# Attention units issued in pairs of a pooled and a local one, batch 1's pooled units spread among local ones, and 41 zero products in place of 76

## The chip, the cores and the metric

The kernel is one program on one core of a Trainium2 chip. The metric is device time in microseconds (us), from the start of the launch to its end. Every run is an execution of the whole program; three runs of the kernel before are shown, and one more execution was profiled. In the rows PE is the matrix engine (TensorE), PEld its weight loads, DVE the vector engine, ACT the scalar engine, POOL the GpSimd engine and SP the engine that issues the DMAs.

## The reference

Three layers run one after the other on 2 x 576 tokens of 512 numbers (8 heads of 64).

```python
# attention, per batch and head
q_d, k_d, v_d = means over groups of 4 positions          # 144 pooled positions
out_d   = softmax(q_d k_d^T / 8) v_d                       # pooled part, repeated 4 times
out_loc = softmax(where(|i-j| < 4, q k^T / 8, -1e9)) v     # local part, a band of 7 keys
x = out_up + out_loc                                       # (1152, 512)
# first FFN
h = x @ w_in;  g = softplus(h);  y = g @ w_out             # 512 -> 2048 -> 512
# 8 experts, each over all tokens
P = exp(y @ w_gate - max), 8 rounds of row and column normalisation
out = sum_e P[:, e] * (relu(y @ w1[e]) @ w2[e])            # 512 -> 1024 -> 512
```

## The kernel before, in words

**The stages.** Attention for both batches comes first, then the first FFN (lines 424 and 464), then the gate and the experts (lines 514 and 563). The experts begin at 337 us and take the rest of the time. The weights of the first FFN arrive as pairs of 32-bit words and are converted in `from_double` (line 115: three ACT, five DVE and one POOL instruction for each of eight pieces); `prep` starts one piece.

**Attention.** There are 8 pooled units and 10 local units for each batch. A pooled unit covers 72 pooled queries of two heads, a local unit 116 (the last ones 112) queries of four heads with a window of 122 keys. A unit has four steps, s1 to s4:

- s1: scores into a bank of PSUM, `pd` (two products over 64 rows, line 284) or `pl` (a mask product in bf16, line 339, and four products over 64 rows, line 347); then DVE finds the negated maximum `nm` (line 270) and ACT the exponentials `e` (line 273).
- s2: transposes of `e` on PE (`ptd` line 299, `ptl` line 359), copied to SBUF by ACT.
- s3: products with the values (`pvd` line 308, `pvl` line 367), then on DVE the sum `rsd`/`rsl`, its reciprocal `rrd`/`rrl` and the scaled result `uld`/`ull` (lines 316 to 320, 373 to 377).
- s4: a transpose back (`pxd` line 325, `pxl` line 383). A pooled unit's result is kept in `upT`; a local unit adds it on DVE (line 389) and POOL writes x (lines 400, 401).

The 64 rows of a head lie in the upper or the lower half of the array: a pooled unit p uses half `p // 2`, a local unit g half `g`. All these banks come from one pool of 6 buffers (`psa`, line 205); the banks of the first FFN and of the zero products come from a pool of 2 (`psm`, line 204).

**The order.** `emit` (line 715) takes units one at a time and issues s1 of the newest unit, s2 of the unit two places earlier, s3 four and s4 six places earlier. Batch 0 and batch 1 each run as four pooled units, then local and pooled ones in turn, then the remaining local ones (line 735). Other work is hung on a place in this list (lines 756 to 764): the loads of batch 1, the pooling of its q and k (`pool_qk`), the `prep` calls, and pieces of the first FFN, the last six of which come after the last unit begins. A scheduler then sets the order of each engine's instructions from this program order and its own estimate of times; every engine runs its list in order.

**Zero products.** `warm` (line 186) multiplies a zero tile of 128 x 128 with 512 zero columns on PE; nothing reads the result. There are 17 at the start, then one behind each of the first 23 steps and behind every second step up to the 95th, 76 in all.

**Batch 1's values.** `load_vd` (line 251) loads v in groups of four positions (`vr`, two DMAs issued by SP), and adds them in two steps (`vs`, line 260, and `vd`, line 262), on DVE for batch 0 and on POOL for batch 1. Each of DVE and POOL waits in its list where such an addition stands until the transfer has landed.

Of the kernel before, what the change touches and what calls it, by code (L numbers as in the profile page):

```python
# [47 lines left out]
AT = (0, 256)  # L48
A11, A12, A22, S1, S2, S3, S4 = range(7)
B11, B21, B22, T1, T2, T3, T4 = range(7)  # L50
STEP = 2
WARM, JALL, JN, NJ = 17, 24, 2, 96
GP = 80
SCALE = 0.125
assert SCALE == D**-0.5
# [20 lines left out]
class Net:  # L76
# [143 lines left out]
    def pool_qk(self, b, p):  # L220

        nc = self.nc

        def sums(t, nm):
            s = self.atp.tile([P, G, 2], F32, tag="ks", name=f"s{nm}{b}{p}", bufs=2)
            v = t.rearrange("p (g f) -> p g f", f=POOLF)
            nc.gpsimd.tensor_tensor(s, v[:, :, 0:2], v[:, :, 2:4], ALU.add)
            nc.gpsimd.tensor_tensor(d, s[:, :, 0], s[:, :, 1], ALU.add)

        q = self.qT[b, p]  # L230
        d = self.atp.tile([P, G], F32, tag="qd", name=f"qd{b}{p}", bufs=NPAIR)
        if b == 0:
            nc.vector.tensor_reduce(
                out=d, in_=q.rearrange("p (g f) -> p g f", f=POOLF), op=ALU.add, axis=AX.X
            )
            nc.scalar.activation(q, q, AF.Copy, scale=SCALE)
        else:
            sums(q, "q")
            nc.gpsimd.tensor_scalar(q, q, SCALE, None, ALU.mult)
        self.qd[b, p] = d  # L240
        d = self.atp.tile([P, G], F32, tag="kd", name=f"kd{b}{p}", bufs=NPAIR)
        sums(self.kT[b, p], "k")
        nc.gpsimd.tensor_scalar(d, d, SCALE / (POOLF * POOLF), None, ALU.mult)
        self.kd[b, p] = d

    def load_vw(self, b, t):
        w = self.vwp.tile([P, H, DA], F32, tag="vw", name=f"vw{b}{t}")
# [3 lines left out]
    def load_vd(self, b):  # L251
        nc = self.nc
        vd = self.atp.tile([GH, 2, H, DA], F32, tag="vd", name=f"vd{b}", bufs=2)
        nc.gpsimd.memset(vd[:, :, :, D:DA], 1.0)
        for hf in range(2):
            r = self.rawp.tile([GP, POOLF, DM], F32, tag="raw", name=f"vr{b}{hf}")
            nc.sync.dma_start(out=r, in_=self.a["vp"][b, hf].rearrange("p (f d) -> p f d", f=POOLF))
            s = self.convp.tile([GH, 2, DM], F32, tag=("ch", "cs")[hf], name=f"vs{b}{hf}", bufs=1)
            e = nc.vector if b == 0 else nc.gpsimd
            e.tensor_tensor(s, r[:GH, 0:2], r[:GH, 2:4], ALU.add)  # L260
            sv = s.rearrange("p f (h d) -> p f h d", h=H)
            e.tensor_tensor(vd[:, hf, :, 0:D], sv[:, 0], sv[:, 1], ALU.add)
        self.vd[b] = vd
        self.upT[b] = self.atp.tile([P, NPAIR, G], F32, tag="upT", name=f"upT{b}", bufs=2)

# [10 lines left out]
    def pooled(self, b, hf, p):  # L276
        nc, ident = self.nc, self.ident
        st = {}
        r = p // 2 * D

        def s1():
            ps = self.psa.tile([P, 512], F32, tag="a", name="pd")[:GH, : 2 * G].rearrange("p (j k) -> p j k", j=2)
            for j in range(2):
                nc.tensor.matmul(
                    ps[:, j],
                    lhsT=self.qd[b, (2 * p + j) % 4][r : r + D, hf * GH : (hf + 1) * GH],
                    rhs=self.kd[b, (2 * p + j) % 4][r : r + D, :],
                    start=True,
                    stop=True,
                )  # L290
# [12 lines left out]

        def s3():
            ps = self.psa.tile([P, 512], F32, tag="a", name="pvd")[:GH, : 2 * DA].rearrange("p (j d) -> p j d", j=2)
            for j in range(2):
                for kh in range(2):
                    nc.tensor.matmul(
                        ps[:, j],
                        lhsT=st["pt"][:, j, kh],  # L310
                        rhs=self.vd[b][:, kh, 2 * p + j],
                        start=(kh == 0),
                        stop=(kh == 1),
                    )
# [12 lines left out]

        return [s1, s2, s3, s4]

    def local(self, b, t, g):  # L330
        nc, ident = self.nc, self.ident
# [2 lines left out]
        nq = min(QT, S - QT * t)  # L334
        mv = OFF.index(QT * t - w0)

        def s1():
            ps = self.psa.tile([P, 512], F32, tag="a", name="pl")[:nq, : 4 * KW].rearrange("p (j k) -> p j k", j=4)
            nc.tensor.matmul(
                ps,  # L340
                lhsT=self.identb[:nq, :nq],
                rhs=self.mask[:nq, mv : mv + 1, :].to_broadcast([nq, 4, KW]),
                start=True,
                stop=False,
            )
            for j in range(4):
                nc.tensor.matmul(
                    ps[:, j],
                    lhsT=self.qT[b, j][g * D : (g + 1) * D, QT * t : QT * t + nq],
                    rhs=self.kT[b, j][g * D : (g + 1) * D, w0 : w0 + KW],  # L350
                    start=False,
                    stop=(j == 3),
                )
            st["e"] = self.softmax_exp(ps, 4, nq, KW, "l")
# [47 lines left out]
                n += m  # L402
            self.ends.append((dve.ins, st["act"].ins))

        return [s1, s2, s3, s4]


    def banks(self, n, name):
# [283 lines left out]
    def run(self):  # L692
# [19 lines left out]
        for t in range(3):  # L712
            self.load_vw(0, t)

        def emit(items, rest):

            live = []
            n = 0
            tail = [y for x in zip([None] * (3 * STEP), rest) for y in x] + rest[3 * STEP :]
            for it in [*items, *tail]:  # L720
                if callable(it):
                    it()
                    continue
                live = [it, *live][: 3 * STEP + 1]
                for k, u in enumerate(live[::STEP]):
                    if u is not None:
                        u[k]()
                        n += 1
                        if n < JALL or n % JN == 0 and n < NJ:
                            self.warm(1)  # L730

        def units(b):
            pooled = [self.pooled(b, hf, p) for hf in range(2) for p in (0, 2, 1, 3)]
            local = [self.local(b, t, g) for t in range(NQT) for g in range(2)]
            return pooled[:4] + [u for z in zip(local, pooled[4:]) for u in z] + local[4:]

        def load_second():

# [9 lines left out]
        def prep(n, lag):  # L748

            with ExitStack() as st:  # L750
                for ins in self.ends[-1 - lag]:
                    st.enter_context(self.tc.issue_after(ins))
                self.prep(n)


        at = {1: [load_second], 9: [load_rest]}
        for p in range(NPAIR):
            at.setdefault(13 + p, []).append(lambda p=p: self.pool_qk(1, p))
        for n, lag, u in zip(range(2 * NFT), (1, 1, 0, 0), (14, 18, 23, 29)):
            at.setdefault(u, []).append(lambda n=n, lag=lag: prep(n, lag))  # L760
        one, two, after = self.l1(0, 0, 1), self.l2(0, 0, 1), self.l1(0, 1, 1)
        for m, u in zip(one + two[:2], (22, 24, 26, 28, 30, 32)):
            at.setdefault(u, []).append(m)
        at[36] = [after[0], after[1], two[2], after[2], after[3], two[3]]
        seq = []
        for n, u in enumerate(units(0) + units(1)):
            seq += at.get(n, []) + [u]

        emit(seq, at[36])
        first = {(0, 0), (0, 1)}  # L770
        stack.close()

# [144 lines left out]
```

## Time and profile before

| what | us |
|---|---|
| median of the three runs | 1096.75 |
| the three runs | 1095.97, 1096.75, 1122.32 |
| the profiled execution, its own time | 1097.38 |
| its span, first to last instruction | 1095.5 |
| PE busy in the span | 1066.1 (97%) |
| DVE busy | 783.6 (72%) |
| ACT busy | 433.8 (40%) |
| POOL busy | 233.1 (21%) |
| attention's last product on PE begins | 125.8 |
| experts' first product on PE begins | 337.1 |

Busy time is the time in which an engine had an instruction under way; products on PE are pipelined, so the time that one takes from PE is read from its start to the start of the next, not from its busy column. The granted clock of PE (PEclk) is a share of full speed: 1.00 is 2.4 GHz, 0.50 is 1.2 GHz. In a row of a timeline "x4" says how many instructions of the same kind stand there together; a product of 32-bit floats is two passes, so "x8" of `pl` are the four products of one unit. The brackets at the end of a row say how long the engine stood idle before it, and what ended that.

### The profile page before, as it was taken

What the parts mean: (1) busy time and instruction counts of PE and PEld (TensorE: products, weight loads), DVE (VectorE), ACT (ScalarE), POOL (GpSimd) and SP (SyncE); (2) the same over time, 40 slices, a digit from 0 to 9 for tenths busy, and PEclk for the clock granted to TensorE, in tenths of its full rate; (3) what the DMA queues carried; (4) which work ended last, traced back from release to release, by engine and by line L of the source; (5) the groups of instructions that cost most, each with busy time, mean ns of one, the idle gap of its engine ahead of it and who ended that gap; (6) DMA issues with size and microseconds to landing.
All of it is one profiled execution on the core that took longest, in us unless ns stands there. A gap on an engine that the chain in (4) does not pass through costs nothing.

```text
span 1095.5 us, 16149 instructions
## 1 busy us (share of the span) xinstructions
PE 1066.1 (97%) x6444; PEld 966.7 (88%) x6444; DVE 783.6 (72%) x1430; ACT 433.8 (40%) x803; POOL 233.1 (21%) x254
## 2 busy tenths in 40 slices
PE   9999889999979999999999999999999999999998
PEld 5888779999969898989989898998989989899897
DVE  4788699999778676958567495774947658486562
ACT  4777667685653341314223141231413314132130
POOL 4972322222064311112021120211102011120000
PEclk9989999999999999999999999999999999999999
DMA  9431033222011111112111121111111111110003
GB/s 284 160 106 59 1 119 113 78 77 77 1 63 54 39 39 39 40 40 76 39 39 39 39 78 39 39 39 39 64 53 39 39 39 43 58 56 1 1 1 86
DMA packets 12906, 63.98 MB, mean 58 GB/s; under 512 B 1632, under 2 KB 1888, under 8 KB 6368
## 3 DMA queue, kind: packets, MB, share of 16 engines
q1 hardware_dynamic: 12832, 62.97, 17.5%
q8 instruction: 50, 0.82, 0.3%
q14 instruction: 24, 0.20, 0.1%
HBM read 60.60 MB, written 2.36 MB: 57 GB/s over the span
## 4 chain that ended last, share of the span: by engine, by line
PE 71%; DVE 6%; issue 1%; ACT 1%; POOL 0%; DVEq 0%
PE po L563 36%; PE pu L514 31%; PE py L464 2%; PE ph L424 2%; DVE l L442 1%; DVE yp L476 0%; DVE acc L584 0%; DVE ch L129 0%; DVE l L443 0%; DVE r L441 0%; DVE a L165 0%; DVE w L180 0%; DVE h L445 0%; DVE cm L126 0%; DVE T L505 0%
## 5 line engine op out<-in xcount | busy, mean ns | idle before, releaser
L563 PE MATMUL po<-w,h 128*128 128x512 f32 x1728 | 396.2, 390 | 0.0
L563 PEld LDWEIGHTS po<-w,h 128*128 128x128 f32 x1728 | 323.4, 188 | 66.5
L514 PE MATMUL pu<-T,a 128*128 128x320 f32 (+1 forms) x2688 | 355.0, 293 | 2.3 <-DVE v L536 1.0
L514 PEld LDWEIGHTS pu<-T,a 128*128 128x128 f32 x2688 | 351.7, 188 | 4.2 <-DVE v L536 1.2
L585 DVE SCALAR_TENSOR_TENSOR acc<-po,prob,acc 128x512 f32<-128x512 f32 x126 | 94.3, 749 | 175.3 <-PE po L563 175.2
L526 ACT ACTIVATE h<-c 128x256 fp32r<-128x256 f32 (+1 forms) x256 | 108.9, 443 | 182.3 <-DVE c L536 181.8
L158 POOL TENSOR_TENSOR s<-raw 128x256 f32<-128x256 f32 x32 | 32.1, 1002 | 537.8 <-DVE a L165 533.8
L179 ACT CAST w<-raw 128x1024 fp32r<-128x1024 f32 x32 | 33.7, 1053 | 276.6 <-PE po L563 270.0
L527 DVE SCALAR_TENSOR_TENSOR h<-c,h 128x256 fp32r<-128x256 f32 (+1 forms) x256 | 125.5, 505 | 1.5 <-ACT h L526 0.9
L464 PE MATMUL py<-h,w 128*128 128x384 f32 x576 | 109.7, 347 | 11.1 <-DVE h L445 5.4
L424 PE MATMUL ph<-x,w 128*128 128x384 f32 x576 | 107.6, 343 | 9.1 <-ACT cm L125 4.7
L464 PEld LDWEIGHTS py<-h,w 128*128 128x128 f32 x576 | 103.8, 194 | 13.9 <-DVE h L445 6.9
L424 PEld LDWEIGHTS ph<-x,w 128*128 128x128 f32 x576 | 102.2, 192 | 11.1 <-issue 5.0
L135 POOL TENSOR_TENSOR w<-cs,ch 128x1024 fp32r<-128x1024 f32 x16 | 42.8, 2676 | 111.8 <-DVE ch L134 72.9
L536 DVE TENSOR_TENSOR c<-v,pu 128x320 f32<-128x320 f32 (+1 forms) x128 | 57.8, 452 | 9.5 <-PE pu L514 6.3
L180 DVE TENSOR_TENSOR w<-raw,w 128x1024 fp32r<-128x1024 f32 x32 | 41.3, 1291 | 32.3 <-ACT w L179 32.3
L165 DVE TENSOR_TENSOR a<-s,a 128x1024 fp32r<-128x1024 f32 x32 | 39.8, 1244 | 1.7 <-ACT a L164 1.7
L534 ACT COPY p<-pu 128x256 f32<-128x256 f32 x64 | 25.1, 393 | 33.9 <-PE pu L514 32.3
L164 ACT CAST a<-s 128x1024 fp32r<-128x1024 f32 x32 | 33.4, 1045 | 3.6 <-POOL s L161 3.6
L441 DVE SCALAR_TENSOR_TENSOR r<-r,e 128x768 f32<-128x768 f32 (+1 forms) x28 | 27.4, 979 | 9.4 <-ACT l L440 9.4
L165 DVE TENSOR_TENSOR a<-raw,a 128x768 fp32r<-128x768 f32 x32 | 30.5, 957 | 3.6 <-ACT a L164 3.6
L536 DVE TENSOR_TENSOR v<-u,pu 128x256 f32<-128x256 f32 x64 | 29.0, 453 | 4.2 <-PE pu L514 1.3
(124 smaller groups left out, 1066.7 us busy)
## 6 DMA issues: line engine op xcount, KB each, us to landing
raw<-in_w SPq DMA_DIRECT2D x48, 1024.0 KB, 4.9
vw<-in_vw SPq DMA_DIRECT2D x10, 260.0 KB, 2.7
vr<-in_vp SPq DMA_DIRECT2D x4, 640.0 KB, 10.6
k<-in_k SPq DMA_DIRECT2D x8, 288.0 KB, 5.5
q<-in_q SPq DMA_DIRECT2D x8, 288.0 KB, 6.3
out<-acc SPq DMA_DIRECT2D x5, 256.0 KB, 2.0
out<-acc SPq DMA_DIRECT2D x8, 128.0 KB, 2.3
maskf<-in_mask SPq DMA_DIRECT2D x1, 183.0 KB, 5.8
```

What stands on the lines that cost most here:

```text
L135: nc.gpsimd.tensor_tensor(w[:, 1], s, h, ALU.mult)
L165: nc.vector.tensor_tensor(w[:, 1, lo:hi], src, split(w[:, 0, lo:hi]), ALU.subtract)
L179: nc.scalar.copy(w[:, 0], raw)
L180: nc.vector.tensor_tensor(w[:, 1], raw, split(w[:, 0]), ALU.subtract)
L424: nc.tensor.matmul(ps[:, i], lhsT=wv[:, a, k, fo : fo + P], rhs=x[:, b, k], start=(n == 0), stop=(n == 3 * KD - 1),)
L464: nc.tensor.matmul(ps[:, a], lhsT=w[:, i, d * P : (d + 1) * P], rhs=h[:, j, f], start=(n == 0), stop=(n == 3 * NFT - 1),)
L514: nc.tensor.matmul(ps, lhsT=w[:, x, a, k], rhs=t[:, y, b, k], start=(m == 0), stop=(m == 5))
L526: nc.scalar.activation(hi, src, AF.Relu)
L527: nc.vector.scalar_tensor_tensor(lo, src, 0.0, split(hi), ALU.max, ALU.subtract)
L536: nc.vector.tensor_tensor(to, src, ps, ALU.add)
L563: nc.tensor.matmul(ps, lhsT=h[i][:, f, at * P : (at + 1) * P], rhs=w[:, j], start=(n == 0), stop=(n == 3 * NFT - 1),)
L585: nc.vector.scalar_tensor_tensor(acc, ps, pe, acc, ALU.mult, ALU.add)
```

## The change

`emit` takes pairs of units. For each place it issues the mask products of the newest pair, then s1 of both its units, s2 of both units one place earlier, s3 of the pair two places and s4 of the pair three places earlier. The pairs are two of pooled units, four of a pooled and a local unit of batch 0, two of local units, eight of a pooled unit of batch 1 and a local unit (the last two local units of batch 0 and the first six of batch 1), and two of local units. In each pair of a pooled and a local unit both use the same half of the array. The pooling of batch 1's q and k, the `prep` calls and the pieces of the first FFN hang on places in the list of pairs, and none is left for after the last one. The zero products fall from 76 to 41. The additions of `load_vd` run on DVE for both batches, and the scalings of kd (both batches) and of batch 1's q run on ACT instead of POOL.

```diff
-STEP = 2
-WARM, JALL, JN, NJ = 17, 24, 2, 96
+WARM, JALL, NJ = 17, 4, 11
...
+        qd, kd = (self.atp.tile([P, G], F32, tag=t, name=f"{t}{b}{p}", bufs=NPAIR) for t in ("qd", "kd"))
         if b == 0:
...
-            nc.scalar.activation(q, q, AF.Copy, scale=SCALE)
         else:
-            sums(q, "q")
-            nc.gpsimd.tensor_scalar(q, q, SCALE, None, ALU.mult)
-        self.qd[b, p] = d
-        d = self.atp.tile([P, G], F32, tag="kd", name=f"kd{b}{p}", bufs=NPAIR)
-        sums(self.kT[b, p], "k")
-        nc.gpsimd.tensor_scalar(d, d, SCALE / (POOLF * POOLF), None, ALU.mult)
-        self.kd[b, p] = d
+            sums(q, qd, "q")
+        sums(self.kT[b, p], kd, "k")
+        nc.scalar.activation(kd, kd, AF.Copy, scale=SCALE / (POOLF * POOLF))
+        nc.scalar.activation(q, q, AF.Copy, scale=SCALE)
+        self.qd[b, p], self.kd[b, p] = qd, kd
...
-            e = nc.vector if b == 0 else nc.gpsimd
-            e.tensor_tensor(s, r[:GH, 0:2], r[:GH, 2:4], ALU.add)
+            nc.vector.tensor_tensor(s, r[:GH, 0:2], r[:GH, 2:4], ALU.add)
             sv = s.rearrange("p f (h d) -> p f h d", h=H)
-            e.tensor_tensor(vd[:, hf, :, 0:D], sv[:, 0], sv[:, 1], ALU.add)
+            nc.vector.tensor_tensor(vd[:, hf, :, 0:D], sv[:, 0], sv[:, 1], ALU.add)
...
-        return [s1, s2, s3, s4]
+        return [None, s1, s2, s3, s4]
...
-        def emit(items, rest):
+        def emit(pairs, before):
 
             live = []
...
+            for n in range(len(pairs) + 3):
+                for m in before.get(n, []):
+                    m()
+                live = [pairs[n] if n < len(pairs) else (), *live][:4]
+                for u in live[0]:
+                    if u[0]:
+                        u[0]()
+                for k, pair in enumerate(live):
+                    for u in pair:
+                        u[k + 1]()
+                    if n < JALL or n < NJ and k % 2:
+                        self.warm(1)
...
-        at = {1: [load_second], 9: [load_rest]}
-        for p in range(NPAIR):
-            at.setdefault(13 + p, []).append(lambda p=p: self.pool_qk(1, p))
-        for n, lag, u in zip(range(2 * NFT), (1, 1, 0, 0), (14, 18, 23, 29)):
-            at.setdefault(u, []).append(lambda n=n, lag=lag: prep(n, lag))
+        (p0, l0), (p1, l1) = units(0), units(1)
+
+        pairs = [(p0[0], p0[1]), (p0[2], p0[3]), *zip(p0[4:], l0), (l0[4], l0[5]), (l0[6], l0[7])]
+        pairs += [*zip(p1, l0[8:] + l1), (l1[6], l1[7]), (l1[8], l1[9])]
+
+        before = {1: [load_second], 5: [load_rest]}
+        for p, n in enumerate((4, 4, 5, 6)):
+            before.setdefault(n, []).append(lambda p=p: self.pool_qk(1, p))
+        for n, lag, u in zip(range(2 * NFT), (1, 1, 0, 0), (7, 9, 11, 14)):
+            before.setdefault(u, []).append(lambda n=n, lag=lag: prep(n, lag))
         one, two, after = self.l1(0, 0, 1), self.l2(0, 0, 1), self.l1(0, 1, 1)
...
+        order = one + two[:2] + [after[0], after[1], two[2], after[2], after[3], two[3]]
+        for m, u in zip(order, (11, 12, 13, 14, 15, 16, 17, 18, 18, 19, 20, 21)):
+            before.setdefault(u, []).append(m)
+        emit(pairs, before)
```

Three places of the engines' lists show what moves. A number behind a name says which buffer it is; "x4" stands for four in a row.

The first is PE's list in batch 0, where pooled and local units stand beside each other. Before, from the mask product of one local unit:

```order
L339 LDWEIGHTS identb
L339 MATMUL pl<-mask,identb 116x488
L347 MATMUL pl<-k_118,q_120 116x122
L347 MATMUL pl<-k_122,q_124 116x122
L347 MATMUL pl<-k_142,q_144 116x122
L347 MATMUL pl<-k_154,q_156 116x122
L359 MATMUL ptl<-ident,e 122x116 x4
L367 MATMUL pvl<-vw_189,ptls 116x65 x4
L195 LDWEIGHTS z
L195 MATMUL pz<-z 128x512
```

Of the change, one pair and the steps of the pairs before it:

```order
L335 LDWEIGHTS identb
L335 MATMUL pl<-mask,identb 116x488
L346 MATMUL pl<-k_118,q_120 116x122
L346 MATMUL pl<-k_122,q_124 116x122
L346 MATMUL pl<-k_142,q_144 116x122
L346 MATMUL pl<-k_154,q_156 116x122
L279 MATMUL pd<-kd_147,qd_146 72x144
L279 MATMUL pd<-kd_159,qd_158 72x144
L294 MATMUL ptd<-ident,e 72x72 x4
L358 MATMUL ptl<-ident,e 122x116 x4
L303 MATMUL pvd<-vd_176,ptds 72x65 x4
L366 MATMUL pvl<-vw_189,ptls 116x65 x4
```

The two products `pd` stand directly behind the four `pl` now, both over the same 64 rows, while before the 64-row products of a pooled and of a local unit were parted by full-height work; the zero products between them are gone.

The second is DVE's list where the values of batch 1 come in. Of the change, from the fifth pooled unit's sum on (`vr_484` and `vr_489` are the two transfers):

```order
L311 TENSOR_SCALAR rsd<-pvd 72x2
L255 TENSOR_TENSOR vs_486<-vr_484 72x1024
L313 RECIPROCAL rrd<-rsd 72x2
L372 TENSOR_SCALAR rsl<-pvl 116x4
L257 TENSOR_TENSOR vd_482<-vs_486 72x8x64
L315 TENSOR_TENSOR uld<-pvd,rrd 72x128
L374 RECIPROCAL rrl<-rsl 116x4
L255 TENSOR_TENSOR vs_491<-vr_489 72x1024
L376 TENSOR_TENSOR ull<-pvl,rrl 116x256
L265 TENSOR_REDUCE nm<-pl 116x4
L265 TENSOR_REDUCE nm<-pd 72x2
```

Before, POOL had these additions:

```order
L239 TENSOR_SCALAR q_208<-q_208 128x576
L260 TENSOR_TENSOR vs_461<-vr_459 72x1024
L228 TENSOR_TENSOR kd_679<-sk_680 128x144
L227 TENSOR_TENSOR sq_746<-q_214 128x288
L260 TENSOR_TENSOR vs_466<-vr_464 72x1024
L262 TENSOR_TENSOR vd_457<-vs_461 72x8x64
```

The additions `vs` and `vd` now stand in DVE's list among the maxima, reciprocals and scaled results of the units under way, where before only POOL waited for the transfers.

The third is PE's list at the first product of the first FFN (`ph`). Of the change:

```order
L335 LDWEIGHTS identb
L335 MATMUL pl<-mask,identb 116x488
L346 MATMUL pl<-k_215,q_216 116x122 x2
L346 MATMUL pl<-k_215,q_222 116x122
L346 MATMUL pl<-k_215,q_225 116x122
L279 MATMUL pd<-kd_500,qd_499 72x144
L279 MATMUL pd<-kd_583,qd_582 72x144
L294 MATMUL ptd<-ident,e 72x72 x4
L358 MATMUL ptl<-ident,e 122x116 x4
L303 MATMUL pvd<-vd_482,ptds 72x65 x4
L423 MATMUL ph<-x_94,w_668 128x384
```

The last zero product of the change is the 113th instruction of PE's list and the first `ph` the 224th; between them stand attention's products alone. Before, zero products reach to 94.0 us and the first `ph` is at 70.17 us.

## Rows read from the trace of the kernel before

**Rows 1.** Busy time by stretch; columns named in its first line.

```profile
core 0: us, PE busy (x) PEld busy (x) DVE busy (x) ACT busy (x) POOL busy (x), PEclk, DMA share, GB/s
0.00:20.00 20.00, 17.51 (x86) 7.95 (x87) 9.67 (x17) 8.17 (x19) 7.29 (x19) 1.00 0.93 270
20.00:57.00 37.00, 37.00 (x319) 30.30 (x317) 27.07 (x71) 25.65 (x75) 32.67 (x33) 1.00 0.60 190
57.00:67.50 10.50, 9.94 (x91) 7.92 (x91) 8.27 (x26) 7.45 (x19) 9.40 (x13) 1.00 0.47 152
67.50:74.30 6.80, 6.80 (x29) 5.66 (x28) 5.84 (x11) 3.32 (x9) 5.49 (x9) 0.50 0.00 0
74.30:125.80 51.50, 51.50 (x398) 45.42 (x396) 37.59 (x98) 34.51 (x94) 16.22 (x23) 1.00 0.16 53
139.00:142.70 3.70, 3.06 (x10) 3.09 (x11) 3.56 (x5) 2.16 (x3) 2.37 (x1) 0.54 0.57 237
337.00:1095.50 758.50, 752.42 (x4486) 682.72 (x4484) 509.05 (x1015) 217.19 (x423) 103.71 (x123) 1.00 0.13 43
```

**Rows 2.** All zero products: minimum, median, maximum ns, first and last start.

```profile
L195 PE MATMUL pz<-z x76: 376/381/650, 1.0 to 94.0; 128*128 128x512 bf16 x76
```

**Rows 3.** PE's timeline 30 to 34 us: start, busy, engine, line, operation, tiles.

```profile
30.64 0.37 PE L339 MATMUL pl<-mask,identb 116*116 116x488 bf16 x1
30.95 1.09 PE L347 MATMUL pl<-k,q 64*116 64x122 f32 x8
31.96 0.61 PE L359 MATMUL ptl<-ident,e 116*122 116x116 f32 x4
32.41 0.94 PE L367 MATMUL pvl<-vw,ptls 122*116 122x65 f32 x8
33.19 0.38 PE L195 MATMUL pz<-z 128*128 128x512 bf16 x1
33.41 0.36 PE L383 MATMUL pxl<-ident,ull 116*128 116x116 f32 x2
```

**Rows 4.** PE's timeline near 9 us, two row halves alternating.

```profile
8.92 0.47 PE L284 MATMUL pd<-kd,qd 64*72 64x144 f32 x4 [0.23 <-POOL kd L243]
9.32 1.68 PE L195 MATMUL pz<-z 128*128 128x512 bf16 x7
```

**Rows 5.** PE's timeline 66 to 71 us, the clock falling.

```profile
66.02 0.68 PE L284 MATMUL pd<-kd,qd 64*72 64x144 f32 x4
66.63 0.44 PE L299 MATMUL ptd<-ident,e 72*72 72x72 f32 x4
66.91 0.68 PE L308 MATMUL pvd<-vd,ptds 72*72 72x65 f32 x8
67.42 0.50 PE L383 MATMUL pxl<-ident,ull 112*128 112x112 f32 x2
67.72 0.61 PE L339 MATMUL pl<-mask,identb 116*116 116x488 bf16 x1
68.26 1.97 PE L347 MATMUL pl<-k,q 64*116 64x122 f32 x8
70.17 0.69 PE L424 MATMUL ph<-x,w 128*128 128x384 f32 x1
```

**Rows 6.** DVE's timeline, and the two landings that POOL waited for.

```profile
14.47 1.22 DVE L260 TENSOR_TENSOR vs<-vr 72x1024 f32<-72x1024 f32 x1 [2.87 <-DMA vr<-in_vp]
...
30.78 0.16 DVE L316 TENSOR_SCALAR rsd<-pvd 72x2 f32<-72x2 f32 x1 [0.80 <-PE pvd L308]
...
L260 POOLq EVENT_SEMAPHORE  x2: 17/17/17, 30.6 to 32.8; - x2
```

**Rows 7.** PE's two long waits after attention.

```profile
132.57 2.38 PE L464 MATMUL py<-h,w 128*128 128x384 f32 x12 [2.02 <-DVE l L443]
139.64 9.94 PE L424 MATMUL ph<-x,w 128*128 128x384 f32 x48 [4.69 <-ACT cm L125]
```

**Rows 8.** ACT's scaling of batch 0's q.

```profile
L236 ACT ACTIVATE q<-q x4: 682/682/684, 5.2 to 10.8; 128x576 f32<-128x576 f32 x4
```

More of the change, by code (lines that the diff above doesn't have):

```diff
@@ L222, in pool_qk, with sums @@
         nc = self.nc
-        def sums(t, nm):
+        def sums(t, d, nm):
             s = self.atp.tile([P, G, 2], F32, tag="ks", name=f"s{nm}{b}{p}", bufs=2)
@@ L230, in pool_qk @@
         q = self.qT[b, p]
-        d = self.atp.tile([P, G], F32, tag="qd", name=f"qd{b}{p}", bufs=NPAIR)
+        qd, kd = (self.atp.tile([P, G], F32, tag=t, name=f"{t}{b}{p}", bufs=NPAIR) for t in ("qd", "kd"))
         if b == 0:
             nc.vector.tensor_reduce(
-                out=d, in_=q.rearrange("p (g f) -> p g f", f=POOLF), op=ALU.add, axis=AX.X
+                out=qd, in_=q.rearrange("p (g f) -> p g f", f=POOLF), op=ALU.add, axis=AX.X
             )
-            nc.scalar.activation(q, q, AF.Copy, scale=SCALE)
         else:
-            sums(q, "q")
-            nc.gpsimd.tensor_scalar(q, q, SCALE, None, ALU.mult)
-        self.qd[b, p] = d
-        d = self.atp.tile([P, G], F32, tag="kd", name=f"kd{b}{p}", bufs=NPAIR)
-        sums(self.kT[b, p], "k")
-        nc.gpsimd.tensor_scalar(d, d, SCALE / (POOLF * POOLF), None, ALU.mult)
-        self.kd[b, p] = d
+            sums(q, qd, "q")
[3 more added lines that the diff above has]
+        self.qd[b, p], self.kd[b, p] = qd, kd
     def load_vw(self, b, t):
@@ L335, in local, with s0 @@
         mv = OFF.index(QT * t - w0)
-        def s1():
+        def s0():
             ps = self.psa.tile([P, 512], F32, tag="a", name="pl")[:nq, : 4 * KW].rearrange("p (j k) -> p j k", j=4)
+            st["ps"] = ps
             nc.tensor.matmul(
@@ L345, in s1 @@
             )
+        def s1():
+            ps = st["ps"]
             for j in range(4):
@@ L403, in s4 @@
             self.ends.append((dve.ins, st["act"].ins))
-        return [s1, s2, s3, s4]
+        return [s0, s1, s2, s3, s4]
     def banks(self, n, name):
@@ L713, in run @@
             self.load_vw(0, t)
-        def emit(items, rest):
+        def emit(pairs, before):
             live = []
[L718 to L730, printed above, removed]
+            for n in range(len(pairs) + 3):
[10 more added lines that the diff above has]
+                        self.warm(1)
+            for n in sorted(n for n in before if n >= len(pairs) + 3):
+                for m in before[n]:
+                    m()
         def units(b):
             pooled = [self.pooled(b, hf, p) for hf in range(2) for p in (0, 2, 1, 3)]
-            local = [self.local(b, t, g) for t in range(NQT) for g in range(2)]
-            return pooled[:4] + [u for z in zip(local, pooled[4:]) for u in z] + local[4:]
+            return pooled, [self.local(b, t, g) for t in range(NQT) for g in range(2)]
         def load_second():
@@ L753, in prep @@
                 self.prep(n)
-        at = {1: [load_second], 9: [load_rest]}
-        for p in range(NPAIR):
-            at.setdefault(13 + p, []).append(lambda p=p: self.pool_qk(1, p))
-        for n, lag, u in zip(range(2 * NFT), (1, 1, 0, 0), (14, 18, 23, 29)):
-            at.setdefault(u, []).append(lambda n=n, lag=lag: prep(n, lag))
-        one, two, after = self.l1(0, 0, 1), self.l2(0, 0, 1), self.l1(0, 1, 1)
[L762 to L769, printed above, removed]
+        (p0, l0), (p1, l1) = units(0), units(1)
[6 more added lines that the diff above has]
+            before.setdefault(u, []).append(lambda n=n, lag=lag: prep(n, lag))
+        one, two, after = self.l1(0, 0, 1), self.l2(0, 0, 1), self.l1(0, 1, 1)
+        order = one + two[:2] + [after[0], after[1], two[2], after[2], after[3], two[3]]
+        for m, u in zip(order, (11, 12, 13, 14, 15, 16, 17, 18, 18, 19, 20, 21)):
+            before.setdefault(u, []).append(m)
+        emit(pairs, before)
         first = {(0, 0), (0, 1)}
```

## The prediction

> **What bounds the kernel now.** I read the busy time by stretches first [rows 1]. PE is busy for 752.42 of the last 758.5 us, which the change leaves as they are; the question is what becomes of the first 140 us. From 20 to 57 us and from 74.3 to 125.8 us PE is never idle: attention is bound by PE's list there, and whatever leaves that list shortens the span. The granted clock is 1.00 in these stretches. From 67.5 to 74.3 us it is 0.50, the lower level of 1.2 GHz, and PE is still busy without a gap: the same products simply take longer. PE's timeline gives the price of each step from one start to the next [rows 3]: mask 0.31, the four `pl` 1.01, the four transposes `ptl` 0.45, `pvl` 0.78, one zero product 0.22 us. At the lower level mask and `pl` take 0.54 and 1.91 instead of 0.31 and 1.01 [rows 3, 5], 1.86 times as long. So two things decide: how many products PE is given, and at which level it runs them.
>
> The sum is made against the profiled execution, 1097.38 us; the median of the runs is 0.6 us below it, too little to correct for.
>
> **Zero products.** 35 of 76 go [rows 2], each 0.22 us of a list without gaps [rows 3]: -7.7 us. Of those that went, some filled waits in the first 20 us, where PE has 2.49 us idle [rows 1]; the bound is therefore -5.2, and I take -7.7 since nearly all stood behind 20 us or in stretches that were full.
>
> **64-row products together.** Twelve pairs now visit the 64-row form once instead of twice. What a visit costs is not a row of its own. The four passes of `pd` take 0.61 us in attention's middle [rows 5] and 0.40 where two units' products alternate between the halves [rows 4]. A saved visit lies between nothing and this difference; I take the whole of it, 12 x 0.21 = -2.5, since the entry that goes is what both rows differ by, bounds 0 and -2.5.
>
> The Trainium skill, page "TensorE: Matmul & The Clock Gate", Part 3 on packing small matmuls, says that products in different row groups of the array run at the same time. The alternating row agrees, with 0.40 against 0.61. By that rule pairs in different halves would gain about as much again; but here both units of a mixed pair use the same half, so I take nothing for it.
>
> **Batch 1's pooled units among local ones.** Before, they ran by themselves with little beside them, and PE stood 0.56 us idle from 57 to 67.5 us [rows 1]; local units now fill this: -0.6. The 6.8 us at the lower level behind it [rows 1] would be 3.7 at the higher: -3.1, if nothing of the kind comes elsewhere.
>
> **Scalings to ACT.** q takes ACT 0.68 us each [rows 8], kd has a quarter of the columns and is bounded by the same: in attention's middle four of each, at most 5.4 us, beside 25.65 us of work in 37 [rows 1]. ACT stays below its capacity; I take 0. If ACT were the last to arrive everywhere, 5.4.
>
> **Additions of batch 1's values to DVE.** This is a new wait. The transfers stand at the same place of SP's list as before, and the landings were at 30.6 and 32.8 us [rows 6]; nothing in the change speeds them. DVE's list puts the first addition behind the fifth pooled unit's `rsd`. Before, that `rsd` started at 30.78 [rows 6]. Up to there PE now has 8 zero products (1.8 us), one `pvl` (0.8) and some smaller things less, so DVE is there at about 27.8 and parks until 30.6. Behind it stand the two additions (1.22 each, [rows 6]), `rrd`, `uld`, `rrl`, `ull` and the maxima of the next pair. `ull` comes at about 35, while PE has work for 27.8 + 0.8 (`pvl`) + 0.2 (`pxd`) + 1.3 (mask, `pl`) + 0.6 (`pd`) + 2.0 (next steps), until about 32.7; then `pxd` and `pxl` wait for `uld` and `ull`. That is some 2.3 us of idle PE, 3 with the handing over between engines. Bounds: 0, if DVE comes late, and 4.5, if the maxima behind it hold up the pair that follows. I take +3. In batch 0 DVE waited in the same way, 2.87 us [rows 6], but there PE had zero products to do.
>
> **The clock.** Behind that gap the list has no zero products until the end of attention, and no full-height work of the FFN until the first `ph`. The trace of before has such a stretch once, and the clock fell at its end, 67.5, after only 0.56 us of idle in 10.5 [rows 1]; after the wait of 4.69 us it was at 0.54 too, while PE was busy for 3.06 of 3.70 us [rows 1, 7]. In the fallen stretch, attention products without a gap from 67.5 to 70.17 [rows 5] did not bring it back; it was up again at 74.3, after `ph` had begun. I therefore expect the fall soon after 32 us and the rise only behind the first `ph`. What stands between the gap and that `ph`, at full clock: eight masks with `pl` (8 x 1.32), four `pd` (0.61), four `ptd` (0.28), eight `ptl` (0.45), four `pvd` (0.51), seven `pvl` (0.78), seven `pxl` (0.30) [rows 3, 5], 27.3 us. At 1.86 times this is 23.5 more; some goes by before the fall: +22. Bounds 12 (it comes back half-way) and 24.
>
> The same page of the Trainium skill, "Why this matters for your kernels", says that idle gaps of TensorE between bursts bring the clock down. The trace agrees with it for the wait of 4.69 us but not for the fall at 67.5, where the idle time is 0.56 us in all. The measurement decides; the rule taken alone gives the rival that the clock holds.
>
> **After attention.** PE waited 2.02 and 4.69 us for DVE's and ACT's work on the FFN's first weights [rows 7]. With attention slower, that work has more time: -3, bounds 0 and -6.7.
>
> **Sum.** -7.7 - 2.5 - 0.6 - 3.1 + 3 + 22 - 3 = +8.1: 1097.4 + 8.1 = 1105.5, written as **1105 us**.
>
> **The rivals.**
> - *The clock falls and stays low to the first `ph`* (the forecast): 1105; from 1092 with the kind bounds (12 us of clock, all of the waits absorbed) to 1114 with the others (24 us, a stall of 4.5, nothing absorbed, nothing from the 64-row products). For it speaks that the one stretch of before without zero products and without `ph` lost the clock. Chance 0.60.
> - *It falls, but returns early*, since PE is busy without a gap behind the fall. For it: after the fall at 139 us PE only had to run on for the clock to return [rows 1, 7], if with full-height products. Against: 2.7 us of dense attention products did not do it [rows 5]. With 9 to 11 us of loss in place of 22: about 1093. Chance 0.12.
> - *The clock holds*, because DVE comes late enough or PSUM's six banks give PE enough to go on. For it: in the first 20 us PE idled 2.49 us and the clock stayed at 1.00 [rows 1]. Against: the zero products stood beside that idle time. Then the sum is -13.9, with the stall of 3 us -10.9: 1083 to 1086, quicker than before. It decides if the gap near 32 us is less than about half a microsecond. Chance 0.20.
> - *The clock falls already near 12 us*, where the first units start and PE waits for loads with fewer zero products to fill in. Then about 15 us more of PE's list (from there to 27.8) run at 1.86 times: +13 on the forecast, 1118, and 1121 if the later waits absorb nothing. Chance 0.08, mostly above the bound of 2%.
>
> That the change does not do what it says is a rival inside each: if putting the 64-row products together saves nothing, 2.5 us are to be added everywhere.
>
> **The numbers.** The predicted time is the likeliest case, 1105. Its own range is 1092 to 1114. The range 1081 to 1114 takes in the early return and the holding clock down to 2 us below the sum, and leaves out the last case and the far ends, about 0.15 in all. Two per cent, about what a measurement of this kernel can tell from no change, is 1075 to 1119: faster by more needs the clock to hold and 8 us more than I can find, 0.02; slower by more is the larger part of the last case and a little of the first, 0.07; within it 0.91.
>
> **What would show it.** In the trace of the change: DVE idle before `vs` from about 28 to 30.6 us with the transfer as its end; PE idle before `pxd` or `pxl` near 32 us; PEclk at 0.50 from then to shortly after the first `ph`; mask and `pl` of a pair at about 2.4 us there and at 1.3 or less at full clock; the waits at the first `py` and the second part of `ph` shorter. The prediction is wrong if PEclk stays at 1.00 between 30 and 65 us, if it is at 0.50 already before 25 us, or if PE loses time in the stretch to a wait for ACT.

## The result, and the profile after

The changed kernel takes 1111.21 us (median of four runs, 1110.91 to 1112.16), against 1097.42 before: a ratio of 1.0117 with a 95% interval of 1.0091 to 1.0143. It is 13.8 us slower; 8 had been forecast. Executions of one kernel differ here by whether, and where, the clock falls in attention: of 92 executions of the kernel before, 62 took 1094 to 1104 us and 30, at a lower mean clock, 1110 to 1139, while every one of the changed kernel took about 1111, and the ratios compare undisturbed runs.

The busy time by stretches, columns as in [rows 1]:

```profile
0.00:20.00 20.00, 16.39 (x89) 7.96 (x90) 8.97 (x17) 9.79 (x26) 4.88 (x15) 1.00 0.93 265
20.00:33.60 13.60, 12.04 (x118) 10.04 (x117) 7.74 (x25) 9.03 (x30) 7.49 (x13) 0.99 0.86 238
33.60:90.40 56.80, 56.29 (x276) 49.58 (x275) 32.92 (x83) 28.42 (x74) 20.41 (x26) 0.50 0.29 96
90.40:140.00 49.60, 48.73 (x384) 43.33 (x384) 34.51 (x91) 34.48 (x95) 15.74 (x21) 0.99 0.16 55
350.70:1109.00 758.30, 752.41 (x4485) 682.72 (x4484) 509.26 (x1015) 217.02 (x423) 102.92 (x123) 1.00 0.13 43
```

The last stretch, from the first product of the experts on, takes 758.3 us where it took 758.5 [rows 1]: all of the difference lies ahead of it, since that product comes at 350.7 us and came at 337.1. From 33.6 to 90.4 us, 56.8 us long, the clock is at 0.50 while PE is busy for 56.29 us; in finer windows the low stretch reaches from 33.2 to 91.3 us, 58 us. Before there were 6.8 such microseconds in attention.

DVE's timeline around the transfers of batch 1's values:

```profile
28.18 0.16 DVE L311 TENSOR_SCALAR rsd<-pvd 72x2 f32<-72x2 f32 x1 [0.75 <-PE pvd L303]
30.89 1.22 DVE L255 TENSOR_TENSOR vs<-vr 72x1024 f32<-72x1024 f32 x1 [2.56 <-DMA vr<-in_vp]
...
32.87 0.28 DVE L315 TENSOR_TENSOR uld<-pvd,rrd 72x128 f32<-72x128 f32 x1
...
34.27 0.41 DVE L376 TENSOR_TENSOR ull<-pvl,rrl 116x256 f32<-116x256 f32 x1
```

DVE is idle for 2.56 us with the transfer as the end of it. `rrd`, `uld` and `ull` stand behind: `uld` starts at 32.87 and `ull` at 34.27; without the wait `uld` would have followed its `rsd` within half a microsecond (0.39 us in the kernel before, 30.78 to 31.17). On PE, a pair at full clock (24.97 to 26.78) and the steps around the wait:

```profile
24.97 0.37 PE L335 MATMUL pl<-mask,identb 116*116 116x488 bf16 x1
25.27 1.09 PE L346 MATMUL pl<-k,q 64*116 64x122 f32 x8
26.20 0.65 PE L279 MATMUL pd<-kd,qd 64*72 64x144 f32 x4
26.78 0.45 PE L294 MATMUL ptd<-ident,e 72*72 72x72 f32 x4
...
29.66 0.37 PE L335 MATMUL pl<-mask,identb 116*116 116x488 bf16 x1 [0.58 <-ACT e L268]
...
31.74 0.56 PE L358 MATMUL ptl<-ident,e 116*122 116x116 f32 x4
33.29 1.20 PE L303 MATMUL pvd<-vd,ptds 72*72 72x65 f32 x8 [0.99 <-DVE rrl L374]
34.82 1.78 PE L366 MATMUL pvl<-vw,ptls 122*116 122x65 f32 x8 [0.34 <-DVE ull L376]
36.40 0.32 PE L320 MATMUL pxd<-ident,uld 72*128 72x72 f32 x1
...
36.90 0.61 PE L335 MATMUL pl<-mask,identb 116*116 116x488 bf16 x1
37.44 1.97 PE L346 MATMUL pl<-k,q 64*116 64x122 f32 x8
39.34 0.66 PE L335 MATMUL pl<-mask,identb 116*116 116x488 bf16 x1
```

In the brackets, PE stands 0.99 and 0.34 us for DVE's late results. Ahead of these it stood 0.58 us for ACT's `e`, which ran behind a scaling of q that the change had moved to ACT:

```profile
28.37 0.70 ACT L239 ACTIVATE q<-q 128x576 f32<-128x576 f32 x1
28.95 0.65 ACT L268 ACTIVATE e<-pd,nm 72x144 f32<-72x144 f32 x2
```

The `pvl` behind takes 1.58 us (34.82 to 36.40) instead of 0.78 [rows 3], and mask and `pl` of the next pair 2.44 (36.90 to 39.34) instead of 1.32: the clock has fallen at the end of the gap of 0.99 us, at 33.2; the 0.34 us come after the fall. It returns at 91.3, after `ph` has come; the `ph` at 88.72 are the first in a row:

```profile
86.35 0.67 PE L423 MATMUL ph<-x,w 128*128 128x384 f32 x1
...
88.72 3.51 PE L423 MATMUL ph<-x,w 128*128 128x384 f32 x12
92.07 0.35 PE L382 MATMUL pxl<-ident,ull 112*128 112x112 f32 x2
```

### The profile page after: what moved, and what is told of

Read it like the earlier page. It is cut to its first block, busy times and chain, and to the rows that moved or that the text cites. A ratio compares the mean times of both kernels' runs of the same rounds, so it can differ in the third digit from the quotient of the medians.

```text
span 1109.1 us, 16098 instructions
## 1 busy us (share of the span) xinstructions
PE 1080.1 (97%) x6409; PEld 983.1 (89%) x6409; DVE 780.2 (70%) x1434; ACT 436.4 (39%) x815; POOL 214.6 (19%) x238
## 4 chain that ended last, share of the span: by engine, by line
PE 70%; DVE 3%; issue 1%; ACT 0%; POOL 0%; DVEq 0%
PE po L562 35%; PE pu L513 30%; PE py L463 2%; PE ph L423 2%; DVE acc L583 0%; DVE a L164 0%; DVE w L179 0%; DVE T L504 0%; PE pg L611 0%; DVE c L535 0%; DVE tc L487 0%; DVE l L442 0%; DVE r L440 0%; DVE h L444 0%; POOL s L158 0%
## 5 line engine op out<-in xcount | busy, mean ns | idle before, releaser
L164 DVE TENSOR_TENSOR a<-raw,a 128x768 fp32r<-128x768 f32 x32 | 30.5, 956 | 3.6 <-ACT a L163 3.6
L346 PEld LDWEIGHTS pl<-k,q 64*116 64x116 f32 (+1 forms) x160 | 24.3, 227 | 8.6 <-issue 8.6
```

The lines of the kernel that those rows point to most:

```text
L164: nc.vector.tensor_tensor(w[:, 1, lo:hi], src, split(w[:, 0, lo:hi]), ALU.subtract)
```

## The experiments

Two theories. **Theory 1**: an idle gap in PE's list lets the clock fall, and attention's products alone do not bring it back; the wait that the change put into DVE's list tears the gap. **Theory 2**: attention's products without zero products among them cannot hold the clock at all.

**Batch 1's additions back on POOL.**

```diff
-            nc.vector.tensor_tensor(s, r[:GH, 0:2], r[:GH, 2:4], ALU.add)
+            e = nc.vector if b == 0 else nc.gpsimd
+            e.tensor_tensor(s, r[:GH, 0:2], r[:GH, 2:4], ALU.add)
```

> The kernel after, with the additions of batch 1's values back on POOL; nothing else changed. Theory 1 (the gap that DVE's wait tears into PE's list near 33 us is what brings the clock down): without the wait there is no gap, PEclk stays at 1.00 from 30 to 90 us, and the time is 1111 - 26 (56.7 us at the lower level) - 3 (the gap), about 1082. Theory 2 (attention's products without zero products among them cannot hold the clock, gap or none): the gap goes, the clock still falls between 25 and 45 us and returns only with the first ph, so 1104 to 1109.

Measured: median 1106.83 us of four runs, 1086.67 to 1109.15. DVE's wait is gone, and the list runs without a gap to 37 us; but there is another. ACT's timeline, and PE's:

```profile
36.07 0.32 ACT L238 ACTIVATE kd<-kd 128x144 f32<-128x144 f32 x1 [3.20 <-POOL kd L227]
36.30 1.10 ACT L269 ACTIVATE e<-pl,nm 116x122 f32<-116x122 f32 x4
```
```profile
39.72 0.37 PE L336 MATMUL pl<-mask,identb 116*116 116x488 bf16 x1 [1.77 <-ACT ptds L297]
40.02 1.97 PE L347 MATMUL pl<-k,q 64*116 64x122 f32 x8
```

POOL, which now waits for the transfer, is late with kd, whose scaling the change had moved to ACT: ACT parks 3.20 us for it with `e` behind, and PE stands 1.77 us. From 40.0 us on `pl` takes 1.90 us: the fall came with the next gap, 7 us later than in the changed kernel. Theory 2's numbers came true (three of the four runs at 1106 to 1109, the fall between 25 and 45 us), but not its condition: a gap stands ahead of the fall. The fourth run, 1086.67, is near the 1082 of theory 1. This run does not decide between the two.

**The 41 zero products held at their places.** `issue_after` queues each behind the last product that is written ahead of it.

```diff
-                        self.warm(1)
+                        self.warm_here(1)
```

> The kernel after with the same 41 zero products, but each held in PE's list behind the step it is written after, so that the last stands just ahead of the first ph instead of at 23.6 us. Theory 1 (the gap does it): the wait of DVE and the gap remain, the clock falls near 34 us; 1100 to 1111. Theory 2 (the zero products hold it): PEclk stays at 1.00 or is back within some us of a fall, about 1085 to 1090, the gap of 3 us remaining.

Measured: median 1101.43 us of six runs, 1090.06 to 1125.71; ratio to the kernel before 0.9944 (0.9911 to 0.9976). Three of the six, at 1090 to 1092, are near where theory 2 had them and below theory 1's 1100 to 1111; no profile shows one of these three. The profiled execution (1125.71) shows something else: its clock falls at 11 us, behind gaps of 0.9 us that the zero products no longer filled, and stays down.

```profile
12.00:100.00 88.00, 88.00 (x425) 72.63 (x425) 44.17 (x107) 39.55 (x113) 25.35 (x38) 0.50 0.40 118
```

Twenty-three zero products, singly and twice in twos, lie in these 88 us without an idle moment of PE. Strewn like this they did not bring the clock back in this execution.

**The kernel before with 41 zero products.**

```diff
-WARM, JALL, JN, NJ = 17, 24, 2, 96
+WARM, JALL, JN, NJ = 17, 24, 2, 25
```

> The kernel before with 41 zero products in place of 76 (17 at the start and one behind each of the first 24 steps), nothing else. Theory 1: there is no wait of DVE, so the clock holds to about 65 us as before; 35 x 0.22 us less, 1089 to 1092. Theory 2: the clock falls some us after the last zero product near 24 us and stays low to the first ph, 1105 to 1120.

Measured: median 1126.09 us, ratio 1.0271 (1.0241 to 1.0301). It is the largest loss of all, in a kernel without any of the moved work. PE's timeline and the stretch behind:

```profile
9.05 0.47 PE L284 MATMUL pd<-kd,qd 64*72 64x144 f32 x4 [1.33 <-POOL kd L243]
...
19.01 0.32 PE L299 MATMUL ptd<-ident,e 72*72 72x72 f32 x2 [1.69 <-ACT e L273]
...
21.46 0.61 PE L339 MATMUL pl<-mask,identb 116*116 116x488 bf16 x1
```
```profile
21.40:97.00 75.60, 71.24 (x345) 58.69 (x344) 33.82 (x89) 32.02 (x87) 40.40 (x50) 0.50 0.34 107
```

Two gaps of 1.33 and 1.69 us, and at 21.2 us the clock is down, until 103 us. The last of the 41 zero products is at 16.9 us, not near 24. The time, above both ranges, fits theory 2 better than 1, whose forecast took the early gaps as harmless, as they had been before (0.23 and 1.27); the place fits theory 1 as well, since the fall again stands behind gaps. This run does not part the two. What the zero products from 19.5 us on had done in the kernel before is seen here by their absence.

**The kernel before with batch 1's additions on DVE.**

```diff
-            e = nc.vector if b == 0 else nc.gpsimd
+            e = nc.vector
```

> The kernel before with batch 1's additions on DVE, with its 76 zero products. Theory 1: the gap near 31 us comes here too (2 to 3 us of idle PE) and with it the fall; with zero products and no ph until 70 us the low stretch is up to 30 us, +10 to +16, 1107 to 1113. Theory 2: the zero products fill in or hold the clock, the gap alone costs 0 to 3, 1096 to 1100.

Measured: ratio 0.9993 (0.9979 to 1.0007), no difference. DVE's wait and the stretch behind it:

```profile
29.92 1.46 DVE L260 TENSOR_TENSOR vs<-vr 72x1024 f32<-72x1024 f32 x1 [1.76 <-DMA vr<-in_vp]
```
```profile
20.00:120.00 100.00, 98.95 (x810) 83.27 (x808) 78.42 (x196) 69.25 (x190) 56.81 (x68) 1.00 0.35 112
```

DVE waits 1.76 us for the transfer here too, and PE has zero products ahead of and behind what is late; it stands 0.34 us for the late `ull`, at 34.57, and nowhere more than 0.37, and the clock is 1.00 from 20 to 120 us. Less stood behind the wait than in the changed kernel (this `uld` was done at 26.9), but in this list the wait costs nothing.

**Additions and scalings of batch 1 back on POOL** (the edit of the first experiment, and `nc.gpsimd.tensor_scalar` for kd and q where b is 1).

> The kernel after, with batch 1's additions and batch 1's scalings of q and kd back on POOL: neither DVE nor ACT then stands behind the transfers of the values; the 41 zero products stay. Theory 1 (a gap in PE's list lets the clock fall, and attention's products alone do not bring it back): between 24 us and the first ph PE has no gap over half a microsecond, PEclk stays at 1.00, about 1080 to 1085. Theory 2 (attention without zero products falls by itself): the clock falls between 25 and 45 us without a gap ahead of it; 1104 to 1110.

Measured: median 1097.99 us, ratio 1.0003 (0.9965 to 1.0041). Three stretches of the profiled execution:

```profile
18.00:30.80 12.80, 12.80 (x69) 9.40 (x68) 4.75 (x14) 4.91 (x16) 8.28 (x11) 0.51 0.93 283
31.00:63.50 32.50, 31.90 (x287) 27.21 (x284) 23.95 (x67) 22.29 (x67) 23.04 (x24) 1.00 0.38 131
64.80:84.00 19.20, 16.53 (x77) 14.55 (x76) 13.07 (x26) 11.44 (x25) 14.53 (x18) 0.50 0.38 124
```
```profile
64.49 0.54 PE L387 MATMUL pxl<-ident,ull 116*128 116x116 f32 x2 [0.51 <-DVE ull L381]
```

From 31 to 63.5 us there is no zero product, no `ph` and hardly a gap, and the clock holds for 32.5 us: theory 2 falls. Ahead of that it had been down since 16.8, in a gap of 1.82 us, and came back at 30.5, after eleven zero products between 17 and 29 us, most of them in twos: more densely strewn than in the execution above that stayed down, though whether that brought it back is not shown. It fell again at 64.6, behind a wait of 0.51 us, so a small gap is enough at times. The time, 1098 us, is in neither range.

**Scalings alone back on POOL.**

> The kernel after with batch 1's scalings alone back on POOL; its additions stay on DVE. Theory 1: DVE's wait remains, and with it the gap near 33 us and the fall: 1108 to 1112. Rival (the moved scalings made the gap): no gap, 1080 to 1086.

Measured: median 1112.06 us, ratio 1.0121 (1.0089 to 1.0153): as the changed kernel.

```profile
32.52 0.70 PE L307 MATMUL pvd<-vd,ptds 72*72 72x65 f32 x8 [1.10 <-DVE rrl L378]
```

The gap is here (1.10 us), with two more of 0.43 and 0.40 behind it, and the clock falls at 35.4 us. The wait of 0.58 us for ACT is not. The scalings were not what made the gap.

**A row of 24 zero products.**

```diff
+                if n == 6:
+                    self.warm_here(24)
```

> The kernel after with 24 more zero products in one unbroken row behind the steps of the seventh pair, near 46 us, where the clock is down. If full-height products in an unbroken row bring the clock back (theory 1, as the first ph did): PEclk 1.00 some us after the row began, to the end of attention; the row costs 24 x 0.22 to 0.44, 5 to 10 us, and about 30 us at the lower level less give 14 back: 1100 to 1107. If only the work of the FFN brings it back: the row costs 10 us, 1121.

Measured: median 1096.9 us, ratio to the kernel before 0.9978 (0.9948 to 1.0008), that is 14 us less than the changed kernel with more work in the list, and 3 us below the range that was expected.

```profile
41.54 6.58 PE L194 MATMUL pz<-z 128*128 128x512 bf16 x24
47.96 0.58 PE L341 MATMUL pl<-mask,identb 116*116 116x488 bf16 x2
```
```profile
50.00:110.00 60.00, 59.17 (x488) 52.02 (x488) 49.08 (x127) 43.76 (x121) 27.14 (x35) 1.00 0.26 80
```

The 24 take 6.42 us (41.54 to 47.96): 24 x 0.22 would be 5.3, and the clock came back within the row, at 44.0 us, where it had been down since 34. Behind it, 60 us of attention and FFN run at 1.00. The edit did one thing more than it says: eight of the 41 zero products, between 18.8 and 23.6 us in the changed kernel, stand behind the row here, from 50.9 to 60.5 us. An unbroken row of full-height products restored the clock, and the FFN was not needed for it.

**Opposite halves** in batch 0's four mixed pairs, on the kernel with additions and scalings on POOL.

```diff
+        p0[4:] = p0[5], p0[4], p0[7], p0[6]
```

> As the run with batch 1's additions and scalings on POOL, and in the four mixed pairs of batch 0 the pooled unit is exchanged for its neighbour, so that its two 64-row products use the other half of the array than the four of the local unit. If products in different halves overlap whenever they stand beside each other: pl and pd of such a pair take about 0.1 to 0.3 us less together. If only alternating products gain: the same within 0.05 us. In the time at most 1 us.

Measured: median 1105.11 us, ratio 1.0024 (0.9977 to 1.0071); the spread of the clock hides a microsecond. The timeline doesn't:

```profile
27.25 0.37 PE L340 MATMUL pl<-mask,identb 116*116 116x488 bf16 x1
27.55 0.77 PE L351 MATMUL pl<-k,q 64*116 64x122 f32 x5
28.06 0.34 PE L284 MATMUL pd<-kd,qd 64*72 64x144 f32 x1
28.16 0.26 PE L351 MATMUL pl<-k,q 64*116 64x122 f32 x1
28.24 0.28 PE L284 MATMUL pd<-kd,qd 64*72 64x144 f32 x1
...
28.70 0.45 PE L299 MATMUL ptd<-ident,e 72*72 72x72 f32 x4
```

From mask to `ptd` it is 1.45 us; with the same half it is 1.81 in the changed kernel (24.97 to 26.78, above) and in the run that this one builds on (30.91 to 32.72). The products of the two units start between each other, though the program issues them one unit after the other.

**Twelve zero products in the gap.**

```diff
+                    if (n, k) == (5, 1):
+                        self.warm_here(12)
```

> The kernel after with 12 more zero products held behind the transposes that end at 32.1 us, where PE then stood idle; DVE's wait stays. Theory 1 (the idle gap lets the clock fall): they fill the gap, cost at most 1 us beyond it, and PEclk stays at 1.00 to the first ph: 1111 less 26 = 1085 to 1088. Rival (it is DVE's wait itself, with all that comes late behind it, that costs the time): the stall is as long and the time stays above 1105.

Measured: median 1095.76 us, ratio 0.9974 (0.9942 to 1.0006). Two rows of PE's timeline in the profiled execution:

```profile
16.76 1.12 PE L300 MATMUL ptd<-ident,e 72*72 72x72 f32 x8 [1.71 <-ACT e L274]
...
38.59 4.36 PE L194 MATMUL pz<-z 128*128 128x512 bf16 x12
```

This execution does not test the gap near 32 us. With the twelve in the list, eleven of the 41 zero products, which stood between 17.5 and 24 us in the changed kernel, stand behind them, from 44.4 to 58 us. The clock falls at 18 us, behind an early gap of 1.71 us with no zero product after it, and DVE comes to the first `vs`, at 34.01, without a wait, so there is no gap to fill. What it shows is the return: the twelve take 4.20 us (38.59 to 42.79), the clock is up at 41.8, within them, and from 46 to 120 us it is 1.00. The 24 us at the lower level, which at 1.86 cost 11, are what keeps the time from the 1085 that was expected.

**The additions held back on DVE**, no product added.

```diff
-        before = {1: [load_second], 5: [load_rest]}
+        before = {1: [load_second], 6: [load_rest]}
...
-            self.load_vd(1)
+            with self.tc.issue_after(self.ends[-1][0]):
+                self.load_vd(1)
```

> The kernel after, no product added: the additions of batch 1's values stay on DVE but are held behind the first local unit's last addition (near 33 us), when the transfers have landed, so DVE no longer parks with rrd, uld and ull behind it. Theory 1: no gap at 32 to 35 us, no fall there, 1082 to 1087, unless the raw weights, whose buffers come free 2 us later, make ACT and DVE park near 40 us and tear a new gap, then 1104 to 1110 with the fall near 40 us.

Measured: median 1089.12 us of ten runs, 1084.23 to 1100.97; ratio 0.9922 (0.9858 to 0.9986). DVE's timeline and the stretch:

```profile
32.33 0.40 DVE L388 TENSOR_TENSOR xf<-pxl,upT 128x232 f32<-128x232 f32 x1
32.65 2.52 DVE L255 TENSOR_TENSOR vs<-vr 72x1024 f32<-72x1024 f32 x2
35.10 0.41 DVE L376 TENSOR_TENSOR ull<-pvl,rrl 116x256 f32<-116x256 f32 x1
```
```profile
20.00:120.00 100.00, 97.02 (x810) 85.71 (x808) 79.40 (x212) 74.84 (x206) 48.61 (x65) 1.00 0.35 112
```

The two `vs` run with no wait ahead of them, and the clock is 1.00 throughout, 41 zero products as in the changed kernel, the last again near 23 us. One edit, which takes the wait out of the head of DVE's list, turns the loss into a gain: five of ten executions take 1084 to 1086 us, one 1093. Four take 1100 to 1101. Gaps of 0.59, 0.90 and 0.77 us are left (PE is idle for 2.98 of 100 us); in the profiled execution none of them lost the clock. The loads of the raw weights move one place later with `load_rest` (33.88 us in place of 32.14); that part was not tried by itself.

**Held back, and those two gaps filled** with 4 and 5 zero products.

> The run with the additions held back, plus 4 zero products behind the steps of the eighth pair and 5 behind those of the tenth, where PE still stood 0.6 to 0.9 us for ACT's exponentials (43.7 and 53.8 us). If these two gaps are what let the clock fall in the executions near 1100 us of that kernel: hardly any execution near 1100 remains, all at 1084 to 1087, which beats both kernels. If the fall comes from the early gap (16.4 us) or a later one: as many near 1100 as before, four in ten.

Measured: median 1086.8 us, 1083.96 to 1091.51 in six runs; ratio 0.9903 (0.9874 to 0.9932). None near 1100; in the profiled execution a next gap of 0.87 us, at 59.9, is left, and from 61.7 to 68.6 us the clock is at 0.50. Six of the 41 zero products, at 20 to 23 us in the run before, stand at 42 to 57 us here, so more than nine fill this stretch. Six executions are few beside four of ten near 1100; that these two gaps were to blame is likely, not shown.

**That gap filled too, and the opposite halves.**

> The run with held additions and two filled gaps, plus 5 zero products behind the steps of the eleventh pair, where PE then waited 0.87 us and the clock fell for about 3 us, and the opposite halves in batch 0's four mixed pairs, which took 1.45 instead of 1.81 us from mask to ptd. If both work as measured: 4 x 0.36 = 1.4 us less, the fall at 60 us seldom, 1083 to 1086 with a median below 1086. If the clock decides by chance at other gaps: a spread as before, 1084 to 1092.

Measured: median 1086.63 us, four of six runs 1084.51 to 1087.22; ratio 0.9884 (0.9857 to 0.9912), some 13 us quicker than the kernel before beside it, and by the medians 25 quicker than the changed one. The profiled execution has 1.00 in every stretch to 120 us. Two of six runs still lost the clock somewhere (1104 and 1116), the median is 0.6 us above what was expected, and the 1.4 us of the halves are not to be told from the spread.

## Why the prediction was right, and where its sizes were off

The forecast (slower by some microseconds, since DVE's wait lets the clock fall until the first `ph`) came true in its mechanism and within its range; the size was 13.8 us where 8.1 were summed.

- **Zero products.** 41 are left, the last at 23.6 us. -7.7 as forecast, taken over and not measured by itself. PE idled 3.61 us in the first 20, where it had been 2.49: +1.1, inside the bound that was given.
- **64-row products together.** Mask to the end of `pd` takes 1.81 us in the pair above; apart, it was 1.32 with 0.61 for `pd` [rows 3, 5], 1.93; with what `ptl` behind gains (0.40 instead of 0.45), about 0.16 a pair, -1.9 instead of -2.5 (worked out, not tried by itself).
- **Batch 1's pooled units, and the fall before.** The stretch at 0.50 that stood from 67.5 to 74.3 us is gone from its place, as forecast (-0.6 and -3.1, taken over).
- **Scalings to ACT.** Taken at 0. PE stood 0.58 us at 29.66 for an `e` behind a moved scaling of q; with batch 1's scalings on POOL this wait is gone. A wait for ACT was one of the prediction's signs of being wrong; it came, small, and is in the next term.
- **DVE's wait.** Forecast from 27.8 to 30.6 us, measured from 28.34 to 30.89. PE lost 1.56 us ahead of 33.6 and 0.51 after: 2.1 where 3 were taken. Of the 2.1, 0.99 and 0.34 are waits for DVE and 0.58 the wait for ACT. For DVE it stood ahead of `pvd` and `pvl`, not of `pxd` and `pxl` as forecast.
- **The clock.** This is the term that was mis-sized: +22 in the sum, measured 58 us at the lower level, PE busy for 57.5 of them, which at 1.86 is 26.6. The products that were counted, from the pair behind the gap to the first `ph`, took 49.45 us (36.90 to 86.35) where the count gives 27.3 x 1.86 = 50.8. What failed is "some goes by before the fall": the fall came in the gap, at 33.2, 3.7 us ahead of the first product counted (+1.5), and the clock came back only 5 us after the first `ph` had begun (+2.3).
- **After attention.** PE's idle time from 90.4 us to the experts is 17.35 us (0.87 + 2.33 + 14.15) where it was 20.24 from 74.3 us on: -2.9, forecast -3.

Together -7.7 + 1.1 - 1.9 - 0.6 - 3.1 + 2.1 + 26.6 - 2.9 = +13.6, and the experts start 13.6 us later. So close a match is in part luck: three terms are taken over from the forecast, and the stretches at the lower level between attention and the experts, 13.7 us before and 17.1 after, are not in the sum.

One argument of the prediction was weaker than its result. It read the fall at 67.5 us as a sign that the clock falls when there are no zero products, whatever the gaps, and set this against the Trainium skill, page "TensorE: Matmul & The Clock Gate", "Why this matters for your kernels", where idle gaps bring the clock down. The stretch of 32.5 us at 1.00 without a zero product, and the kernel with its additions held back, side with the Trainium skill: every fall whose surroundings were read here stands behind gaps, that at 67.5 us too, where the last zero product is at 55.85 us:

```profile
65.57 0.41 PE L383 MATMUL pxl<-ident,ull 112*128 112x112 f32 x2 [0.41 <-ACT e L273]
```

In size they do not side with it: the falls stand behind gaps of 0.41 to 1.82 us, shorter than those the Trainium skill warns of there, and the measurement decides. Nor does a gap decide alone. One of 1.27 us before (at 18.46 us), of 0.90 us with the additions held back and of 1.31 us in the last run lost nothing, and where the gaps were longest without a fall zero products stood around them. How long a gap must be, and what must stand around it, was not settled; chance may have a part.

The rule of the same page of the Trainium skill, Part 3, that products in different row groups run at the same time, is agreed with by 1.45 against 1.81 us. The prediction put about 0.21 us on it for a pair; it is 0.36.

Left open: which gap loses the clock in the executions near 1100 us of the kernels that beat both. Shown is that DVE's wait costs the changed kernel its clock; that it does so by PE's gap is the reading that fits the runs best, but the run that was to fill this gap had no gap to fill.

## What to carry to other kernels

An addition that waits for a transfer can cost its whole queue: ask what stands behind it in that engine's list, and whether the bottleneck has anything to do meanwhile. Where a fall of the clock turns a gap of one or two microseconds into tens, count gaps before busy time, and put the wait where the data has already landed (here one edit, from 1111 to 1089 us in the median). To recover a clock that has fallen, put filler work in an unbroken row: that worked both times it was tried, while 23 strewn products did not. And look where a filler pushes the others: here added zero products moved up to eleven of the old ones 20 us and more down the list.

## What the runs showed of the hardware

- Attention's products can run on at either level of the clock: nearly without a gap they held 1.00 for 32.5 us in one execution and stayed at 0.50 for 49 us in another (36.9 to 86.35), or for 88 us with 23 zero products strewn among them.
- Twelve and 24 zero products in a row, 4.2 and 6.4 us of PE, brought it back in the two profiled executions that had them while the clock was down.
- 64-row products in opposite halves of the array start between each other though the program issues them one unit after the other: 0.36 us of 1.81 for six of them.
